# Block-sparse attention with float32 products and gathered key blocks, split units for experts 0 and 1, and seven block products in the first layer of experts 3 to 7

## The chip, the cores and the metric

The kernel runs on one core of a Trainium2 chip. The core has a matrix engine (TensorE, PE in the rows; its weight loads are PEld), a vector engine (DVE), a scalar engine (ACT), a general one (POOL), a synchronization engine (SP) and 16 DMA engines. DMAs are issued from the queues of SP, ACT and POOL. The metric is device time in microseconds, lower is better.

## What is computed

Sparse attention over 4 batches, 8 heads, 768 positions of 64 features, then a layer of 8 experts of which each of the 3072 rows takes its top two:

```python
    mask = np.abs(blk_i - blk_j) <= window          # blocks of 32, window 1
    mask = mask | (blk_i == 0) | (blk_j == 0) | (blk_i == n_blocks - 1) | (blk_j == n_blocks - 1)
    for qb in range(n_blocks):                      # 24 blocks
        for kb in sampled_blocks[qb]:               # 3 each
            mask[qb * block:(qb + 1) * block, kb * block:(kb + 1) * block] = True
    scores = np.where(mask, scores, -1000000000.0)
...
    attn = attn / (np.sum(attn, axis=-1, keepdims=True) + 1e-09)
    return np.matmul(attn, v).astype(np.float32)
...
    noisy_logits = logits + noise_scale * noise
    top2 = np.argpartition(-noisy_logits, 2, axis=1)[:, :2]
...
            h = np.maximum(x[mask] @ w1[e], 0.0)
            out[mask] += top2_w[mask, k, None] * (h @ w2[e])
```

`x` is the attention's output with 512 features a row; `w1[e]` is 512 x 1024, `w2[e]` 1024 x 512. So a query block of the middle sees at most eight key blocks (first, last, three neighbours, three sampled), and the two end blocks of queries see all 24. A wrong choice of expert changes a whole row, so the scores need more than float16's accuracy.

## The kernel before

**Attention** (`Attention`) goes through 192 steps: 4 batches x 8 heads x 6 row tiles of 128. Each step treats all 768 keys; the mask is added by extra rows of the contraction. Values of float32 are split into a float16 high and low half, and products are made of two or three float16 products. A step has these parts: `max_mm` (L227) computes rough scores of 128 rows x 768 keys in two matmuls, and `max_red` (L234, DVE) takes the row maximum; `exp` computes exact scores turned the other way (keys on partitions) in four matmuls (L255, L256) and `exp` of them on ACT (L257) as 32-bit patterns, of which `halve` (L262, DVE) makes two float16 numbers each; `av` multiplies them with the values, 18 matmuls of 64 or 65 columns (L288). After six steps of a head `av_end` copies, normalizes and rounds the result (L300 to L317, ACT, DVE, POOL). Loading and splitting q, k and v (L160 to L198) uses ACT and POOL and DMA transposes on SP's queue.

**Router** (`Router.run`) runs as a list of small steps that are drawn one by one between the attention's; per batch it computes the gates, takes the top two, counts places with matmuls against a triangle of ones, and scatters (row, weight) into a table in DRAM (`slots`, L647).

**Experts** (`Experts`). A unit is a stretch of one expert's rows: first 640 rows of expert 0 out of batches 0 to 2, which can start while batch 3 is still being routed, then 224 rows of expert 0 from batch 3, then 816 rows for each of experts 1 to 7. For a unit, `meta` and `indices` read the table, `gather` fetches rows (POOL), `xpose` turns them with a DMA transpose (SP), `mm1` computes the first layer in 8 groups of 12 products (high-high, high-low, low-high of four input blocks; L816, 408 columns for units of 816), ACT and DVE make the rounded half `hh` and the rest `hl` (L821, L822), `mm2` the second layer, 24 matmuls of 512 columns for each 128 rows (L836), and `finish` scales, adds what the other expert has left there (`gather_prev`, L782) and scatters to `out` (L864, L866). Of the rows beyond the last full 128, `mm2` computes the transpose (L845) and `turn` turns it with float32 transposes (L855). Weights come as 8 pieces of 512 KB per expert (`load_piece`, SP) and are split by ACT and DVE (L729, L730) during the unit before.

Each engine works through its instructions in the order of the program; the order is written out by hand: `steps` and the final loop call the parts one after the other. An instruction waits for semaphores of those whose data it needs, and what stands behind it on its engine waits too. PSUM has 8 banks; a pool's number of buffers says how far its writer may run ahead of its reader.

## Time and profile before

| | |
|---|---|
| time, median of 3 runs | 1052.07 us (1046.19 to 1056.2) |
| span of the profiled execution, first to last instruction | 1028.6 us |
| busy share of the span: PE, DVE, ACT, POOL | 87%, 55%, 37%, 35% |
| granted TensorE clock, mean | 0.971 |
| bytes moved by DMA | 156.40 MB |

Of the profiled execution the span alone is given, no time beside it: the timed runs include what lies around the first and the last instruction, the span does not. An average over the whole span mixes two stages, attention and the experts, so the views by window are of more use. A matmul's busy time includes its way through the array; how fast matmuls follow each other is read from their starts.

### The profile page before, as it was taken

What the parts mean: (1) busy time and instruction counts of PE and PEld (TensorE: products, weight loads), DVE (VectorE), ACT (ScalarE), POOL (GpSimd) and SP (SyncE); (2) the same over time, 40 slices, a digit from 0 to 9 for tenths busy, and PEclk for the clock granted to TensorE, in tenths of its full rate; (3) what the DMA queues carried; (4) which work ended last, traced back from release to release, by engine and by line L of the source; (5) the groups of instructions that cost most, each with busy time, mean ns of one, the idle gap of its engine ahead of it and who ended that gap; (6) DMA issues with size and microseconds to landing.
All of it is one profiled execution on the core that took longest, in us unless ns stands there. A gap on an engine that the chain in (4) does not pass through costs nothing. (4 is left out here: it accounts for less than half of the span.)

```text
span 1028.6 us, 20575 instructions
## 1 busy us (share of the span) xinstructions
PE 891.4 (87%) x8413; PEld 529.1 (51%) x8413; DVE 563.1 (55%) x1039; ACT 377.1 (37%) x754; POOL 355.9 (35%) x399
## 2 busy tenths in 40 slices
PE   3788897779878878997899999989989999899993
PEld 1465565556555545653645455545544544454551
DVE  7699989979988977464123333323323323233320
ACT  2466666556656645432113123122122221221200
POOL 3142322542255253333360251342512513512211
PEclk9899999999999999998999999999999999999997
DMA  8988986899989766736957376295494483653200
GB/s 183 182 171 183 219 196 159 154 164 179 182 178 167 144 133 145 200 85 176 165 130 199 109 174 184 90 196 168 131 184 141 124 214 104 182 144 110 69 34 33
DMA packets 238073, 156.40 MB, mean 152 GB/s; under 512 B 172577, under 2 KB 213793, under 8 KB 237968
## 3 DMA queue, kind: packets, MB, share of 16 engines
q1 hardware_dynamic: 206816, 91.45, 44.1%
q0 software_dynamic: 14256, 39.58, 13.2%
q10 hardware_dynamic: 16896, 23.95, 8.6%
q8 instruction: 68, 1.11, 0.5%
q14 instruction: 37, 0.30, 0.1%
HBM read 79.62 MB, written 26.32 MB: 103 GB/s over the span
## 5 line engine op out<-in xcount | busy, mean ns | idle before, releaser
L257 ACT ACTIVATE p<-pe 128x384 int32<-128x384 f32 x384 | 183.0, 491 | 152.8 <-PE pe L256 125.7
L822 DVE SCALAR_TENSOR_TENSOR hl<-ph,hh 128x408 f16<-128x408 f32 (+2 forms) x136 | 75.6, 560 | 211.2 <-ACT hh L821 177.0
L866 POOL DMA_INDIRECT out_dram<-y,mt x56 | 73.0, 1304 | 323.9 <-DVE y L864 196.4
L234 DVE TENSOR_REDUCE m<-pm 128x1 f32<-128x768 f32 x192 | 181.6, 948 | 1.4 <-PE pm L227 1.4
L821 ACT ACTIVATE hh<-ph 128x408 f16<-128x408 f32 (+2 forms) x136 | 66.2, 492 | 301.9 <-PE ph L816 210.2
L227 PE MATMUL pm<-k,q 88*128 88x384 f16 x384 | 98.5, 340 | 67.8 <-DVE m L234 42.6
L262 DVE TENSOR_SCALAR p<-p 128x1536 f16<-128x1536 uint16 x192 | 124.7, 650 | 45.9 <-ACT p L257 44.0
L288 PEld LDWEIGHTS <-p 128*128 128x128 f16 x3456 | 130.4, 100 | 25.8 <-issue 4.7
L255 PE MATMUL pe<-q,k 128*128 128x384 f16 x384 | 128.7, 335 | 7.7 <-ACT p L257 4.4
L256 PE MATMUL pe<-q,k 128*128 128x384 f16 x384 | 127.9, 333 | 6.7 <-DMA q<-qb 6.7
L288 PE MATMUL po<-vx,p 128*128 128x65 f16 x1152 | 125.3, 197 | 1.8 <-issue 1.4
L288 PE MATMUL po<-vb,p 128*128 128x65 f16 x1152 | 125.8, 196 | 0.9 <-issue 0.9
L288 PE MATMUL po<-vl,p 128*128 128x64 f16 x1152 | 125.5, 195 | 0.0
L836 PEld LDWEIGHTS <-hh 128*128 128x128 f16 x768 | 75.0, 98 | 93.8 <-issue 8.8
L864 DVE SCALAR_TENSOR_TENSOR y<-py,mt,pv 128x512 f32<-128x512 f32 x48 | 36.0, 751 | 153.9 <-PE py L836 145.0
L816 PE MATMUL ph<-xta,w1hb 128*128 128x408 f16 x512 | 110.9, 339 | 9.6 <-DVE hl L822 8.7
L816 PE MATMUL ph<-xtb,w1ha 128*128 128x408 f16 (+1 forms) x448 | 95.3, 334 | 14.2 <-DVE hl L822 12.3
L227 PEld LDWEIGHTS <-q 88*128 88x128 f16 x384 | 37.9, 100 | 122.1 <-issue 96.7
L816 PEld LDWEIGHTS <-w1ha 128*128 128x128 f16 x576 | 57.4, 100 | 52.9 <-issue 18.4
L836 PE MATMUL py<-w2ha,hh 128*128 128x512 f16 x192 | 73.9, 385 | 4.9 <-DVE y L864 3.9
L816 PEld LDWEIGHTS <-w1hb 128*128 128x128 f16 x512 | 50.2, 98 | 49.7 <-issue 12.3
L836 PE MATMUL py<-w2la,hh 128*128 128x512 f16 x192 | 73.8, 384 | 0.3 <-issue 0.3
(172 smaller groups left out, 1404.3 us busy)
## 6 DMA issues: line engine op xcount, KB each, us to landing
wraw<-in_moe_w_dram SPq DMA_DIRECT2D x64, 512.0 KB
q<-q SPq DMA_DIRECT2D x32, 192.0 KB
raw_v<-in_v_dram ACTq DMA_DIRECT2D x16, 384.0 KB
out_dram<-zero ACTq DMA_DIRECT2D x8, 768.0 KB
x_rows<-x SPq DMA_DIRECT2D x16, 384.0 KB
raw_k<-in_k_dram ACTq DMA_DIRECT2D x14, 384.0 KB
raw_q<-in_q_dram ACTq DMA_DIRECT2D x14, 384.0 KB
k<-k SPq DMA_DIRECT2D x17, 192.0 KB
```

The lines of the kernel that those rows point to most:

```text
L227: self.nc.tensor.matmul(pm[:, c, 0:384], r["q3"][0:K, h, t, :], r["k2"][0:K, h, 3 * c:3 * c + 3, :], start=True, stop=True)
L234: self.nc.vector.tensor_reduce(self.st[g]["m", h][:, t:t + 1], pm[:, :, 0:384], axis=AX.XY, op=ALU.max)
L255: nc.tensor.matmul(pe[:, 0:384], r["k1"][:, h, c, :], r["q1"][:, h, t, :], start=True, stop=False)
L256: nc.tensor.matmul(pe[:, 0:384], r["k2"][:, h, c, :], r["q2", h][:, t, :], start=False, stop=True)
L257: nc.scalar.activation(p32[:, t].rearrange("p t c -> p (t c)"), pe[:, 0:384], AF.Exp, scale=0.125)
L262: self.nc.vector.tensor_scalar(p.rearrange("p t c w -> p (t c w)"), p32.bitcast(U16).rearrange("p t c -> p (t c)"), HC, None, op0=ALU.mult)
L288: self.nc.tensor.matmul(o, p[:, t, :, w], v, start=first and i == 0, stop=last and i == 2, skip_group_check=True)
L816: nc.tensor.matmul(ph[:, b, 0:m], w[wt][:, kb, fs], r["xt"][:, kb, a, o:o + m], start=i == 0, stop=i == last)
L821: nc.scalar.activation(hv, ph[:, b, 0:m], AF.Relu)
L822: nc.vector.scalar_tensor_tensor(self.hl[:, f, o:o + m], ph[:, b, 0:m], 0.0, hv, op0=ALU.max, op1=ALU.subtract)
L836: nc.tensor.matmul(py, h[:, f, o], w[x][:, f, :], start=i == 0, stop=i == last)
L866: nc.gpsimd.indirect_dma_start(out=self.out, out_offset=bass.IndirectOffsetOnAxis(ap=r["mt"][0:m, c, 0:1], axis=0), in_=y[0:m], in_offset= ...
```

## The change

**Attention** is written anew. The host lays the inputs out in other orders (queries and keys turned, 32-row blocks together, values with their neighbours side by side); this is outside the time measured. The work is a list of 64 items: per batch 12 of kind "q" (row tile t of 128 queries = 4 blocks, and f, half of the heads) and 4 of kind "g" (the 64 queries of the first and last block against all 768 keys for two head pairs). All matmuls and transposes of attention are float32, with no split.

- `prefetch_k`: POOL copies the three sampled key blocks of each query block behind the keys, 128 x 128 each, from an address held in a register. `prefetch_v`: SP loads the neighbours' values in one DMA and each sampled block in a DMA of 64 KB at a register's address, 11 on average per row tile. A sampled block that is seen already gets weight 0 (`blocks`, `weigh`).
- `scores`: for each of 4 heads and 4 query blocks a matmul of 64 rows, 32 stationary columns and 192 moving ones (three neighbours, three sampled), and 4 matmuls of 64 columns for the end blocks. A head of a pair uses the upper or the lower 64 partitions and a bank of its own.
- `soft`: row maxima (DVE) and `exp` (ACT, 4 of 256). `turn`: PE transposes them, 8 of 128 x 128 in the same banks, copied out by DVE and ACT. `av`: 32 matmuls of 68 columns, each for 32 queries. `norm`: three DVE operations. `high`, `low`: float16 halves on ACT and POOL. `turn_x`: PE instead of DMA transposes the rows for the router, DVE copies them; they go through the one bank `ps_o` that `av` uses.
- The row store, the zero fill of the output and all loads are issued by SP; the zero fill moves from attention to the first unit of the experts.

**Units.** Experts 0 and 1 both have a unit of 640 rows out of the first three batches and one of 224; the short ones come third and fourth. The units of 640 and 224 that come first for their rows (0 and 2) do not read the output back.

**Seven products.** For experts 3 to 7 the first layer's four input blocks and 816 rows are taken as 2 x 2 blocks and multiplied with seven products in place of eight: 28 products of 6 matmuls of 408 columns. DVE and ACT make sums of weights (`weight_sums`), sums and differences of rows (`row_sums`, `row_differences`, `row_high`, `row_low`) during the unit before, and add the products up (`layer1_fast`). PSUM banks: three "pa", two "pc", two "pd", one "pr". The output DMAs of one unit no longer wait for each other.

On PE in the middle of attention, rows of before (`k`, `q` are halves of keys and queries, `p` the exponentials, `vx`, `vl`, `vb` the values' halves):

```order
L227 LDWEIGHTS q_2318
L227 MATMUL pm<-k_100,q_2318 128x384
L255 LDWEIGHTS k_1827
L255 MATMUL pe<-q_1980,k_1827 128x384
L256 LDWEIGHTS k_102
L256 MATMUL pe<-q_2317,k_102 128x384
L288 LDWEIGHTS p_2466
L288 MATMUL po<-vx_104,p_2466 128x65
L288 LDWEIGHTS p_2466
L288 MATMUL po<-vl_110,p_2466 128x64
L288 LDWEIGHTS p_2466
L288 MATMUL po<-vb_107,p_2466 128x65
```

and of the change, one q item (`kk` keys, `q` queries, `va` and `vb` values, `ptr` turned exponentials; `x16` counts equal neighbours):

```order
L298 MATMUL ps<-r_ident,p 128x128 x8
L225 MATMUL ps<-kk_106,q 32x192 x16
L225 MATMUL ps<-kk_106,q 128x64 x4
L320 MATMUL po<-va_99,ptr 32x68 x4
L320 MATMUL po<-vb_102,ptr 32x68 x4
L320 MATMUL po<-va_99,ptr 32x68 x4
L320 MATMUL po<-vb_102,ptr 32x68 x4
```

The two rough matmuls and the four exact ones of a row tile are gone; 16 narrow ones and 8 transposes stand in their place for four heads, and the 18 value matmuls of a tile become 32 with 32 rows of output each.

On DVE in the middle of attention, before (`m` maxima, `p` exponentials, `rc` and `xr` normalization):

```order
L305 RECIPROCAL rc<-rc 128x6
L308 TENSOR_TENSOR xr<-xo,rc 128x384
L262 TENSOR_SCALAR p_4207<-p_4177 128x1536
L234 TENSOR_REDUCE m<-pm 128x1
L262 TENSOR_SCALAR p_4241<-p_4210 128x1536
L234 TENSOR_REDUCE m<-pm 128x1
L262 TENSOR_SCALAR p_4278<-p_4248 128x1536
```

and in the change, about two items (`ps` scores or their transposes, `po` the bank of the outputs, `r_xT` the turned rows):

```order
L302 COPY ptr<-ps 128x512
L391 COPY r_xT<-po 128x1024
L271 TENSOR_REDUCE m<-ps 128x2 x2
L327 TENSOR_SCALAR rc<-po 128x4
L328 RECIPROCAL rc<-rc 128x4
L330 TENSOR_TENSOR xr<-po,rc 128x256
L302 COPY ptr<-ps 128x512
L271 TENSOR_REDUCE m<-ps 128x2 x2
L307 MEMSET ptr 32x4x32
```

A row tile and head had one maximum over 768 and one scaling over 1536 halves; an item of four heads has one copy of 512, two maxima over 512 and three operations of normalization, every second one a copy of 1024 too.

On DVE in the first layer of an expert, before (`hl` low halves, `w2la` weights' low halves, `gi` indices, `y` output rows):

```order
L822 SCALAR_TENSOR_TENSOR hl<-ph,hh 128x408 x4
L730 SCALAR_TENSOR_TENSOR w2la<-wraw,w2ha 128x1024
L752 TENSOR_SCALAR gi<-mt 128x6
L752 TENSOR_SCALAR gi<-mt 48x1
L822 SCALAR_TENSOR_TENSOR hl<-ph,hh 128x408 x12
L864 SCALAR_TENSOR_TENSOR y<-py,mt,pv 128x512
```

and in the change, first layer of a unit with seven products (`pa`, `pc`, `pd` banks, `ta`, `tc` partial sums, `xf` row sums, `w_...` weights):

```order
L980 TENSOR_TENSOR tc<-pa,tc 128x408
L963 SCALAR_TENSOR_TENSOR hl<-tc,hh 128x816
L980 TENSOR_TENSOR tc<-pd,tc 128x408
L963 SCALAR_TENSOR_TENSOR hl<-pa,hh 128x408
L980 TENSOR_TENSOR ta<-pc,ta 128x408
L963 SCALAR_TENSOR_TENSOR hl<-tc,hh 128x816
L963 SCALAR_TENSOR_TENSOR hl<-ta,hh 128x408
L825 SCALAR_TENSOR_TENSOR w_11313<-wraw,w_11313 128x1024
L836 TENSOR_TENSOR xf<-xta 128x816
```

Sixteen low halves with little between them become additions, low halves, weight halves and row sums in one sequence.

The diff, cut to the parts above:

```diff
-        pm = self.ps_m.tile([P, 2, 512], F32, name="pm")
-        for c in range(2):
-            self.nc.tensor.matmul(pm[:, c, 0:384], r["q3"][0:K, h, t, :], r["k2"][0:K, h, 3 * c:3 * c + 3, :],
-                                  start=True, stop=True)
...
-        nc.tensor.matmul(pe[:, 0:384], r["k1"][:, h, c, :], r["q1"][:, h, t, :], start=True, stop=False)
-        nc.tensor.matmul(pe[:, 0:384], r["k2"][:, h, c, :], r["q2", h][:, t, :], start=False, stop=True)
-        nc.scalar.activation(p32[:, t].rearrange("p t c -> p (t c)"), pe[:, 0:384], AF.Exp, scale=0.125)
...
-        for t in range(self.T):
-            first, last = c == 0 and t == 0, c == self.T - 1 and t == self.T - 1
-            for i, (o, w, v) in enumerate(((po[:, t, :], 1, vh[:, h, c, :]), (po[:, t, 0:D], 1, vl[:, h, c, :]),
-                                           (po[:, t, :], 0, vb[:, h, c, :]))):
-                self.nc.tensor.matmul(o, p[:, t, :, w], v, start=first and i == 0, stop=last and i == 2,
-                                      skip_group_check=True)
...
+    def prefetch_k(self, b, t):
+        nc, kk = self.nc, self.kk[b % 2]
+        js = self.real(t)
+        v = self.numbers(self.ri, t, mybir.EngineType.Pool, self.NB - 1)
+        flat = kk.rearrange("p n c -> p (n c)")
+        for j in js:
+            for n in range(3):
+                nc.gpsimd.tensor_copy(kk[:, self.row(t, j) + n], flat[:, bass.ds(v[j, n] * P, P)])
...
+        part = lambda x: x.rearrange("p (j c) -> p j c", j=J)[:, js[0]:js[-1] + 1]
+        nc.sync.dma_start(va[0:96, js[0]:js[-1] + 1, 0:HD], part(self.vw[b, t]))
+        v = self.numbers(self.mi, t, mybir.EngineType.SP, self.NB)
+        vv = self.vx[b].rearrange("(n p) c -> n p c", p=32)
+        for j in js:
+            for n, d in enumerate((va[96:128, j], vb[0:32, j], vb[32:64, j])):
+                nc.sync.dma_start(d[:, 0:HD], vv[bass.ds(v[j, n], 1)].rearrange("o p c -> (o p) c"))
...
+    def scores(self, it):
...
+        q = self.st["q", b, t]
+        self.st[it, "s"] = [self.bank() for _ in range(2)]
+        s = [x.rearrange("p (e c) -> p e c", e=2) for x in self.st[it, "s"]]
+        for e in range(2):
+            p = 2 * f + e
+            for j in range(self.NJ):
+                blk = min(max(t * self.NJ + j - 1, 0), NB - 3)
+                for par in range(2):
+                    w = kk[head(par), blk:blk + 3, p]
+                    step = (self.row(t, self.slot(t, j)) - blk) * P
+                    w = bass.AP(tensor=w.tensor, offset=w.offset, ap=[list(w.ap[0]), [step, 2]] + [list(a) for a in w.ap[1:]])
+                    mm(s[par][32 * j:32 * j + 32, e, 0:192], q[head(par), p, 32 * j:32 * j + 32], w)
+        for e in range(2):
+            p = 2 * f + e
+            for par in range(2):
+                mm(s[par][:, e, 192:256], q[head(par), p, :], kk[head(par), 0:NB:NB - 1, p])
+    def soft(self, it):
...
+        m = self.sm.tile([P, 2, 2], F32, name="m")
+        p = self.st[it, "p"] = self.pp.tile([P, 4, 256], F32, name="p")
+        for par in range(2):
+            nc.vector.tensor_reduce(m[:, par], s[par].rearrange("p (e c) -> p e c", e=2), axis=AX.X, op=ALU.max, negate=True)
+        for par in range(2):
+            for e in range(2):
+                nc.scalar.activation(p[:, 2 * e + par], s[par][:, 256 * e:256 * e + 256], AF.Exp, bias=m[:, par, e:e + 1])
+    def av(self, it):
...
+        va, vb = self.st["v", b, t]
+        o = self.st[it, "o"] = self.psum()[:, 0:4 * W].rearrange("p (h w) -> p h w", w=W)
+        for h in range(4):
+            for x, v in ((0, va), (1, vb)):
+                for j in range(self.NJ):
+                    nc.tensor.matmul(o[32 * j:32 * j + 32, h], d[:, h % 2, h // 2, x, 32 * j:32 * j + 32],
+                                     self.values(v[:, self.slot(t, j)], 4 * f + h), start=h == 0 and x == 0,
+                                     stop=h == 3 and x == 1, skip_group_check=True)
+    def norm(self, o, n):
+        nc, D = self.nc, self.D
+        rc = self.sm.tile([P, n], F32, name="rc")
+        nc.vector.tensor_scalar(rc, o[:, :, D], 1e-9 / XS, None, op0=ALU.add)
+        nc.vector.reciprocal(rc, rc)
+        x = self.xp.tile([P, n, D], F32, name="xr", bufs=3)
+        nc.vector.tensor_tensor(x, o[:, :, 0:D], rc[:, :, None].to_broadcast([P, n, D]), op=ALU.mult)
+        return x
...
+    def turn_x(self, xT, b, t):
+        nc = self.nc
+        x = self.x_tile(b, t).rearrange("p k a c -> p (k a) c")
+        o = self.psum().bitcast(F16).rearrange("p (c k) -> p c k", c=2 * self.NP)
+        for c in range(2 * self.NP):
+            nc.tensor.transpose(o[:, c], x[:, c], self.ident16)
+        nc.vector.tensor_copy(xT[:, t].rearrange("p k a c -> p (k a) c"), o)
...
-        self.units = [(0, 0, CA), (E, 0, CB)] + [(e, e, C) for e in range(1, E)]
+        self.units = [(0, 0, CA), (1, 1, CA), (E + 1, 1, CB), (E, 0, CB)] + [(e, e, C) for e in range(NH, E)]
+PRODUCTS = [(int(a), int(b)) for a, b in ("01 11 02 06 12 21 07 16 05 17 04 15 03 14 22 27 26 31 13 24 36 25 37 35 "
+                                           "32 34 23 33").split()]
+HOOKS = (3, 6, 10, 13, 17, 20, 23, 27)
...
+    def weight_sums(self, e, i):
...
+        a = self.st["wraw", e, i].rearrange("p (s c) -> p s c", s=4)
+        c = self.st["ws", e, i] = self.sp.tile([P, 4, 2 * P], F32, name="ws")
+        tt = lambda x, y, z, op: nc.vector.tensor_tensor(x, y, z, op=op)
+        tt(c[:, 0], a[:, 3], a[:, 2], ALU.add)
+        tt(c[:, 1], c[:, 0], a[:, 0], ALU.subtract)
+        tt(c[:, 2], a[:, 0], a[:, 3], ALU.subtract)
+        tt(c[:, 3], a[:, 1], c[:, 1], ALU.subtract)
...
+    def layer1_fast(self, u, hook):
...
+        t = lambda i: (lambda s, a: tb[:, s, a, i])
+        terms = {1: (0, x(0, 0)), 2: (1, x(1, 0)), 3: (6, x(1, 1)), 4: (2, t(2)), 5: (3, t(0)), 6: (4, t(3)), 7: (5, t(1))}
...
+        for n, (g, p) in enumerate(PRODUCTS):
+            w = self.w1b[self.units[u][1], g]
+            slot, mv = terms[p]
+            if p in tail:
+                banks[g, p] = self.bank(tail[p])
+            o = banks[g, owner[p]][:, 0:M]
+            i = 0
+            for s in range(2):
+                for wt, a in ((0, 0), (0, 1), (1, 0)):
+                    nc.tensor.matmul(o, w[:, wt, slot, s * P:s * P + P], mv(s, a), start=i == 0 and p in tail,
+                                     stop=i == 5, skip_group_check=True)
+                    i += 1
...
+            if p == 1:
+                once[g] = self.tp.tile([P, M], F32, name="ta")
+                keep(once[g], ba)
+            if p in (6, 7):
+                if g not in both:
+                    both[g] = self.tp.tile([P, 2, M], F32, name="tc")
+                keep(both[g][:, p - 6], bd if p == 7 else ba)
+            if p == 2:
+                tt(once[g], bc[:, 0:M], once[g])
+                self.high(g, 0, M, once[g])
+                later.append((g, 0, M, once[g]))
+            seen = set(PRODUCTS[:n + 1])
+            if p == 4:
+                tt(both[g][:, 0], bd[:, 0:M], both[g][:, 0])
+            if p in (5, 7) and {(g, 5), (g, 7)} <= seen:
+                tt(both[g][:, 1], ba[:, 0:M], both[g][:, 1])
+            if p in (4, 5, 7) and {(g, 4), (g, 5), (g, 7)} <= seen:
+                v = both[g].rearrange("p k c -> p (k c)")
+                self.high(4 + g, 0, C, v)
+                later.append((4 + g, 0, C, v))
+            if p == 3:
+                self.high(g, M, M, ba[:, 0:M])
+                later.append((g, M, M, ba[:, 0:M]))
...
+        for p in r.setdefault("done", []):
+            self.tc.declare_no_dep(d.ins, p.ins, reason="a unit has every row once")
```

## Rows read from the trace of the kernel before

**Rows 1.** The page: span.
```profile
span 1028.6 us, 20575 instructions
```
**Rows 2.** Windows by stage: start:end, us, busy and (count) per engine, clock, DMA, GB/s.
```profile
60.00:400.00 340.00, 280.23 (x4169) 194.51 (x4168) 309.26 (x607) 206.99 (x466) 132.40 (x166) 0.98 0.85 169
452.00:487.50 35.50, 29.72 (x124) 12.47 (x122) 14.91 (x21) 9.43 (x11) 17.96 (x27) 0.90 0.59 137
585.20:1012.00 426.80, 410.63 (x2623) 215.88 (x2620) 136.83 (x199) 91.50 (x143) 136.81 (x120) 0.98 0.52 138
1012.00:1028.60 16.60, 0.00 (x0) 0.00 (x0) 0.64 (x1) 0.00 (x0) 0.98 (x1) 0.65 0.05 19
```
**Rows 3.** Tiles po and ph: duration ns min/median/max, first and last start (us).
```profile
L288 PE MATMUL po<-vx,p x1152: 190/194/262, 33.6 to 419.5; 128*128 128x65 f16 x192
...
L816 PE MATMUL ph<-xtb,w1ha x448: 256/336/548, 488.0 to 909.8; 128*128 128x408 f16 x128, 128*128 128x224 f16 x22
...
L816 PE MATMUL ph<-xta,w1ha x128: 296/299/474, 419.6 to 452.0; 128*128 128x320 f16 x128
```
**Rows 4.** The page, costliest groups: count, busy us, mean ns, idle before.
```profile
L234 DVE TENSOR_REDUCE m<-pm 128x1 f32<-128x768 f32 x192 | 181.6, 948 | 1.4 <-PE pm L227 1.4
...
L262 DVE TENSOR_SCALAR p<-p 128x1536 f16<-128x1536 uint16 x192 | 124.7, 650 | 45.9 <-ACT p L257 44.0
```
**Rows 5.** Groups by form, DVE.
```profile
L822 DVE SCALAR_TENSOR_TENSOR hl<-ph,hh 128x408 f16<-128x408 f32 x112 | 64.8, 582 | 188.1 <-ACT hh L821 160.8 <-issue 27.3
L864 DVE SCALAR_TENSOR_TENSOR y<-py,mt,pv 128x512 f32<-128x512 f32 x48 | 36.0, 751 | 153.9 <-PE py L836 145.0 <-remote 8.4 <-DVE w2lb L730 0.5
...
L730 DVE SCALAR_TENSOR_TENSOR w2la<-wraw,w2ha 128x1024 f16<-128x1024 f32 x16 | 19.6, 1223 | 1.9 <-ACT w2ha L729 1.5 <-issue 0.4
...
L308 DVE TENSOR_TENSOR xr<-xo,rc 128x384 f32<-128x384 f32 x32 | 17.8, 558 | 2.8
...
L303 DVE TENSOR_SCALAR rc<-xo 128x6 f32<-128x6 f32 x32 | 5.2, 161 | 1.3 <-ACT xo L300 1.3
...
L521 DVE COPY r_lc<-pe 128x192 f32<-128x192 f32 x3 | 1.0, 346 | 0.0
```
**Rows 6.** Timelines of PE: start, us (of merged neighbours), shapes, count; three stretches.
```profile
99.66 0.19 PE L288 MATMUL po<-vx,p 128*128 128x65 f16 x1
99.69 0.19 PE L288 MATMUL po<-vl,p 128*128 128x64 f16 x1
...
513.70 0.60 PE L855 MATMUL pr<-r_ident,yt 128*96 128x128 f32 x4
514.14 0.64 PE L816 MATMUL ph<-xta,w1hb 128*128 128x408 f16 x2
...
586.16 0.85 PE L816 MATMUL ph<-xtb,w1ha 128*128 128x408 f16 x4
...
587.20 0.85 PE L816 MATMUL ph<-xtb,w1ha 128*128 128x408 f16 x4
```
**Rows 7.** Groups by form, ACT.
```profile
L257 ACT ACTIVATE p<-pe 128x384 int32<-128x384 f32 x384 | 183.0, 491 | 152.8 <-PE pe L256 125.7 <-PE pm L227 7.5 <-remote 7.0
...
L821 ACT ACTIVATE hh<-ph 128x224 f16<-128x224 f32 x8 | 2.7, 356 | 16.9 <-PE ph L816 12.3 <-remote 4.6
```
**Rows 8.** Groups by form, POOL.
```profile
L647 POOL DMA_INDIRECT slots<-r_pay,r_sl x48 | 51.5, 1072 | 39.4 <-DVE r_ot L639 30.2 <-issue 7.7 <-DVE r_pay L636 1.2
...
L194 POOL TENSOR_TENSOR ka<-raw_k,ka 128x384 f16<-128x384 f32 x28 | 27.0, 963 | 37.0 <-ACT ka L192 33.0 <-DMA q<-qb 2.7 <-issue 1.2
...
masks.py:197 POOL MEMSET r_ident<- 128x128 f32 x1 | 0.2, 199 | 0.0
```
**Rows 9.** Timeline of SP's queue: start, us that issuing took; two stretches.
```profile
1.23 0.42 SPq L330 DMA_DIRECT2D raw_k<-in_k_dram  x1
...
315.57 1.14 SPq L498 DMA_DIRECT2D x_rows<-x  x1
```
**Rows 10.** The page, DMA queues: packets, MB, share of 16 engines.
```profile
q0 software_dynamic: 14256, 39.58, 13.2%
```

## What the change should do

> **What bounds the kernel now.** I read the stage windows first, then each engine's groups. The last value matmul (L288) starts at 419.5 us and the first expert matmul (L816) at 419.6 [rows 3], so the span of 1028.6 us [rows 1] is 419.5 us of attention, 592.5 us of experts (to 1012.0) and a tail of 16.6 in which PE does nothing [rows 2]. The reader is to see in the window 60:400 which engine is full: DVE is busy 309.3 of 340 us (91%), PE 280.2 (82%), ACT 207.0 (61%). Two DVE groups make nearly all of it: the row maximum L234 (948 ns) and the scaling L262 (650 ns), both 192 times [rows 4], together 306.8 us. Attention is bound by DVE, with PE close behind. In the experts the order is reversed: in 585.2:1012 PE is busy 410.6 of 426.8 us, DVE 136.8 [rows 2]. There PE is the bound, and only fewer columns or fewer stalls shorten it. The timed median, 1052.07 us, lies 23.4 above the profiled span; I add that to every sum.
>
> **Attention, DVE.** The change removes L234 and L262 altogether, and most of the scores: 192 row tiles of 768 keys become 48 items ("q": 128 queries, 4 heads, 256 keys) and 16 items for the queries of the two end blocks ("g"). Prices: a DVE read of PSUM costs 346 ns for 192 elements (L521) and 948 for 768 [rows 4, 5], hence 145 ns + 1.045 ns per element: 680 ns for 512, 546 for 384, 1215 for 1024; the product L308 (558 ns for 384) gives about 425 for 256 [rows 5]. Per q item: one copy of 512 (0.68), two maxima over 512 (1.36), the normalization (two small operations of 0.16 to 0.18 and the 0.43), half of a 1024 copy (0.61): 3.42 us. A third of a g item (two maxima of 384, one small operation, one copy: 1.93) is 0.64. The router, whose work is not changed, has some 50 small DVE operations a batch at 0.16 to 0.2 us, like L303 [rows 5]: 9 us, for three of four batches within attention 27 / 48 = 0.57. Small copies and memsets: 0.25. Sum 4.9 us an item, 48 x 4.9 = 235 us, in place of 306.8 for two groups alone.
>
> **Attention, PE.** Everything is now float32, and no row shows a float32 product; the nearest are the four float32 transposes L855, which take 513.70 to 514.14, 109 ns each for 128 columns, 0.85 ns a column. A float16 column costs 0.42 (six matmuls of 408 in 1.035 us, 172.5 ns each), and a matmul of 65 columns still follows the last after 31 ns [rows 6]. Per item there are 16 score matmuls of 192 columns, 4 of 64, 32 value matmuls of 68, a third of 4 x 384 and 5.3 x 68 for the end blocks: 6380 columns, besides 10.7 transposes (1.16 us) and 4 float16 ones (0.22). One after the other at 0.85 ns that is 6.8 us an item. But a score matmul uses 64 rows and 32 columns of the array, and its neighbours use the others and other PSUM banks or partitions; a value matmul uses 32 columns. If they run side by side (8, 2, 4, 2 and 2 at a time) 1493 columns are left, 2.65 us. The matmuls of before use 128 rows (L227: 88) and all 128 columns (the 128*128 of [rows 6]), so the trace decides nothing. I take the middle of the two ends, 4.7 us: just under DVE.
>
> By the Trainium skill ("TensorEngine Tiling (Array Packing)", Key Properties) tiles of the array load weights and multiply independently and in parallel; no run here shows that yet. By it PE would take 2.65 us and DVE alone would bound; without it, PE bounds at 6.8 (the second rival below).
>
> **Attention, the feeders.** ACT: 384 elements take 491 ns, 224 take 356 [rows 7], so 383 for 256: four exponentials, one copy of 512, one rounding, and shares of the end blocks' work come to 3.5 us, hidden under DVE. POOL copies 264 key blocks of 128 x 128 at a register's address (5.5 an item). The nearest rows are a memset of that size (199 ns) and a two-input operation on 384 elements (963) [rows 8]; I take 0.45 with its register work, nearer the memset: 2.5 us, and 2.5 more for scaling, low halves, weights and the slot DMAs (1.07 us each): 5.0, level with DVE. SP issues about 7.4 DMAs an item, 11 per 128 queries at register addresses. An issue took 0.42 us at the start and 1.14 in full attention [rows 9]; at 0.6 that is 4.4 us. The moved bytes are 6.3 MB of keys, 6.3 of queries, 17.3 of neighbour values, 17.3 of sampled ones, 6.3 stored and about 3 others, 56 MB; queue q0 moved 39.58 MB in 13.2% of 1028.6 us [rows 10], 291 GB/s, so 56 MB want 192 us: hidden if attention takes 260.
>
> **Attention, sum.** DVE was busy 91% when it was the bound; 235 / 0.91 = 258. Before it, 12 us until the keys (1.6 MB, 6 us) and block numbers are there and three items are in flight; before, the first value matmul starts at 33.6 us [rows 3]. After it 8 us for the last item, whose turned rows now go through PE ahead of the first expert matmul: a chain of some eight short operations with their waits. 278 us, against 419.5.
>
> **Experts.** A unit of 816 rows took 71.1 us in the mean of seven (514.1 to 1012.0 [rows 2, 6]). Seven products of half size in place of eight: 168 first-layer matmuls of 408 columns instead of 192, 24 x 0.1725 = 4.1 us less for each of five units [rows 6]. The price is on DVE. Per such unit: 12 additions of 408 (0.58 like L822), the low halves (4 x (0.58 + 1.0 + 0.58)), weight sums (16 of 256, 0.42) and the longer weight splits (0.95 + 1.22 x 2 for each quarter), row sums, differences and low halves (about 12), seven L864 of 0.75 [rows 5]: 54 us in 67, where before it is busy 32%. In the first layer alone 26 us of DVE stand against 29 of PE. The banks (three "pa", two "pc", two "pd") let PE run about four products ahead, so I leave the remaining stalls as large as before, 4 us a unit. The unit of 640 rows takes 68.4 us before (419.6 to 488.0 [rows 3]) for 51.9 of PE work: 26.0 and 25.9. I take 60 for the first (the eight fills of the output, 6.3 MB, move here from attention), 54 for the second, whose rows and weights come under the first, 21 for each short one (18 of work; 26 before, when it waited for the last batch's table). Sum: 60 + 54 + 42 + 71 + 5 x 67 = 562 us, against 592.5. The waits between a unit's output DMAs are declared away; the tail hardly sees it, since the last DMA waits for the last y.
>
> Total: 278 + 562 + 16.6 = 857 us of span, 880 with the 23.4.
>
> **Rivals.**
> *Products in four passes, one at a time (slower).* The kernel before gets its accuracy from float16 halves, three products for one (L816). If the array does the same inside a float32 product with all four, a column costs 4 x 0.42 = 1.69 ns; without overlap an item takes 12.2 us of PE, attention 48 x 12.2 + 20 = 606, the whole 1208 us. It decides from 9.0 us an item (attention 450 us), 1.2 ns a column in series. For it: no row shows overlap. Against it: transposes show half that price. The Trainium skill ("FP8 and Floating Point Precision", TensorE Precision Notes) does state four passes for true float32, with nothing on tiles.
> *PE bounds, still faster.* At 0.85 ns in series 6.8 us an item: 326 + 20 + 562 + 17 + 23 = 948. Four passes side by side, 3.9 us, would be hidden; at half clock 7.8 us: 996. For the half clock: before, PE at 82% was granted 0.98, but 0.90 in 452:487.5 where it stood still [rows 2], and it will stand still in each item.
> *The feeders bound.* POOL copies at 963 ns (5.3 + 2.5 = 7.8 us an item) or SP issues at 1.14 (8.4): 374 to 403 + 20, 996 to 1025 us; at 0.6 a copy, 920.
> *Seven products gain nothing.* DVE at 26 of 29 us holds the banks back and the 4.1 us are lost: 900 us, inside the range.
>
> **Numbers.** 58% for DVE-bound attention near 880 (own range 830 to 930); 20% for PE as a bound that stays under 1040; 10% for the feeders; 12% for the serial four passes. The floor is DVE without loss (235 + 20) and the experts at their PE work (521): 816. So 825 to 1000 leaves out the slow rival, the worst of the feeders and a little below. This kernel can tell about 1% from no change: faster by more 0.85, within 0.03, slower 0.12.
>
> **What would show it.** Right: attention ends near 280 us with DVE above 85% there; value matmuls of one item starting a few tens of ns apart; five units near 67 us with first layers near 31. Wrong: PE above 95% and DVE under 60% in attention (either PE rival, told apart by the start-to-start time of the score matmuls and the granted clock); PE's score matmuls waiting for POOL's key copies or value matmuls for SP's DMAs; first layers of 35 us or more with PE waiting for DVE additions.

## The result, and the profile after

The changed kernel took 921.59 us in the median (919.55 to 921.78), the kernel before 1051.28 beside it; the ratio is 0.8806, 95% interval 0.8745 to 0.8866. In a second comparison on the chip it took 909.72 beside 1032.86, ratio 0.8817 (0.8773 to 0.8860). The forecast was 880, range 825 to 1000. Executions of one kernel lie up to 3% apart here (the kernel before: 1026 to 1056), so stages are compared inside profiles, and times only with runs taken beside them.

The profiled execution took 921.78 us, its span is 919.8. The page's first lines, and its line on the queue that brings instructions (packets, MB, share of 16 engines):

```profile
span 919.8 us, 25194 instructions
PE 823.3 (90%) x10119; PEld 520.1 (57%) x10119; DVE 538.3 (59%) x1151; ACT 357.6 (39%) x666; POOL 380.5 (41%) x662
...
q8 instruction: 81, 1.33, 0.7%
```

Windows by stage (columns as in [rows 2]): attention in full flow, its last stretch, all of the experts, the five units with seven products:

```profile
60.00:330.00 270.00, 225.51 (x5201) 172.00 (x5189) 165.59 (x480) 135.92 (x301) 140.61 (x375) 0.94 0.69 165
330.00:351.90 21.90, 14.30 (x281) 12.36 (x282) 8.62 (x26) 3.23 (x8) 6.43 (x9) 0.58 0.90 173
351.90:903.70 551.80, 536.95 (x3616) 301.56 (x3615) 327.33 (x547) 184.66 (x289) 203.95 (x176) 0.98 0.60 160
588.30:903.70 315.40, 315.19 (x2062) 167.00 (x2060) 224.91 (x335) 125.17 (x185) 118.75 (x92) 1.00 0.52 143
```

Attention ends at 351.9 us (419.6 before, [rows 3]); the forecast was 278. The experts take 551.8 (592.5 before; forecast 562), the tail 16.1 (16.6). So the experts came out a little better than forecast and attention ended 74 us later. And DVE, which was to be full, is busy 165.6 of 270 us (61%; 91% before, [rows 2]), PE 225.5 (84%). No engine is full. The last window shows the opposite picture: PE 315.19 of 315.40 us, at full clock.

The values' and the turned scores' groups (duration min/median/max, first and last start):

```profile
L320 PE MATMUL po<-va,ptr x1536: 219/223/323, 26.5 to 343.6; 128*32 128x68 f32 x192
...
L391 DVE COPY r_xT<-po x24: 673/692/692, 56.9 to 351.1; 128x1024 f16<-128x1024 f16 x24
...
L271 DVE TENSOR_REDUCE m<-ps x96: 672/681/692, 18.6 to 328.5; 128x2 f32<-128x512 f32 x96
L302 DVE COPY ptr<-ps x48: 675/682/693, 22.2 to 336.4; 128x512 f32<-128x512 f32 x48
```

`va` has 768 matmuls in the program and 1536 records here: a float32 product appears as two. PE's timeline in the middle of attention (start, us, shapes, count, idle time before and its releaser):

```profile
149.71 0.96 PE L225 MATMUL ps<-kk,q 64*32 64x192 f32 x16
150.60 0.33 PE L320 MATMUL po<-va,ptr 128*32 128x68 f32 x8
150.74 0.30 PE L320 MATMUL po<-vb,ptr 128*32 128x68 f32 x8
150.86 0.30 PE L320 MATMUL po<-va,ptr 128*32 128x68 f32 x8
...
152.11 0.27 PE L346 MATMUL pog<-va,pgt 96*64 96x68 f32 x1
152.66 0.30 PE L346 MATMUL pog<-va,pgt 96*64 96x68 f32 x2 [0.28 <-issue]
153.43 0.28 PE L346 MATMUL pog<-va,pgt 96*64 96x68 f32 x2 [0.46 <-issue]
154.17 1.05 PE L346 MATMUL pog<-va,pgt 96*64 96x68 f32 x27 [0.46 <-issue]
155.15 1.09 PE L298 MATMUL ps<-r_ident,p 128*128 128x128 f32 x8
```

Two things are to be seen. Eight value records take 0.12 us: four start 7 ns apart (one for each 32 columns of the array), the next four 59 ns after the first. That is 0.87 ns a column for each record, four records at a time. By the Trainium skill ("TensorEngine Tiling (Array Packing)", Key Properties) tiles load and multiply in parallel; the trace agrees, and the second experiment shows it by undoing it. Then, at 152 us, matmuls that need nothing new come two at a time with 0.45 us of nothing between. The profile puts that idle time down to "issue": it sees no semaphore that PE waits for. POOL's timeline has this beside it:

```profile
151.35 0.99 POOL L716 DMA_INDIRECT slots<-r_pay,r_sl  x1 [0.16 <-issue]
152.34 0.09 POOL L715 MEMSET r_spacer<- 1x1 f32 x1
152.65 0.98 POOL L716 DMA_INDIRECT slots<-r_pay,r_sl  x1 [0.22 <-issue]
153.66 0.64 POOL L166 TENSOR_SCALAR q<-q 128x512 f32<-128x512 f32 x1
```

PE's waits in attention, from 60 to 330 us (total us, times, longest):

```profile
PE po L320 <- issue: 25.2, 39, 3.2
PE pog L346 <- issue: 6.8, 18, 0.5
PE po L662 <- DVE xr L330: 4.0, 3, 1.9
```

No such idle time has a place in the prediction. Summed over the records from 30 us to attention's end, PE has 38.3 us of idle time before matmuls that wait for no semaphore, in 68 pieces: 55 pieces under 0.6 us (20.1 us), 50 of them within half a microsecond of an indirect DMA of POOL, and 13 longer ones (18.2 us, the longest 3.2). The kernel before has 2.3 us of it. The experiments start there.

### The profile page after: what moved, and what is told of

Its sections match the earlier page's. It is cut to its first block, busy times and chain, and to the rows that moved or that the text cites. A ratio compares the mean times of both kernels' runs of the same rounds, so it can differ in the third digit from the quotient of the medians.

```text
span 919.8 us, 25194 instructions
## 1 busy us (share of the span) xinstructions
PE 823.3 (90%) x10119; PEld 520.1 (57%) x10119; DVE 538.3 (59%) x1151; ACT 357.6 (39%) x666; POOL 380.5 (41%) x662
## 3 DMA queue, kind: packets, MB, share of 16 engines
q8 instruction: 81, 1.33, 0.7%
## 4 chain that ended last, share of the span: by engine, by line
PE 76%; DVE 7%; issue 6%; DMA 3%; another core or an unknown queue 3%; ACT 2%; SPq 1%; POOL 1%; POOLq 0%; DVEq 0%
PE pc L1038 24%; PE pa L991 9%; PE ps L225 9%; PE po L320 7%; PE pd L991 5%; PE ps L298 4%; PE pa L952 4%; PE pc L1047 3%; PE pog L346 3%; PE pc L991 2%; PE pd L952 2%; DVE m L271 2%; PE ps L286 2%; PE po L390 2%
## 5 line engine op out<-in xcount | busy, mean ns | idle before, releaser
L1038 PE MATMUL pc<-w,hh 128*128 128x512 f16 x768 | 230.1, 381 | 0.0
L1038 PE MATMUL pc<-w,hl 128*128 128x512 f16 x384 | 146.3, 381 | 0.0
L991 PEld LDWEIGHTS <-w 128*128 128x128 f16 x840 | 82.2, 98 | 63.1
L274 ACT ACTIVATE p<-ps,m 128x256 f32<-128x256 f32 x192 | 75.4, 475 | 70.0 <-DVE m L271 59.0
L271 DVE TENSOR_REDUCE m<-ps 128x2 f32<-128x512 f32 x96 | 61.8, 684 | 44.5 <-PE ps L225 37.7
L225 PE MATMUL ps<-kk,q 64*32 64x192 f32 (+1 forms) x1920 | 75.3, 329 | 4.7 <-issue 4.0
L894 POOL DMA_INDIRECT xg<-x_rows,gi x56 | 68.7, 1227 | 23.2 <-issue 15.3
L320 PE MATMUL po<-vb,ptr 128*32 128x68 f32 x1536 | 63.9, 233 | 13.9 <-issue 13.5
L825 DVE SCALAR_TENSOR_TENSOR w<-wraw,w 128x1024 f16<-128x1024 f32 (+1 forms) x58 | 65.1, 1126 | 18.9 <-ACT w L821 16.2
L186 POOL COPY kk<-kk 128x128 f32 x264 | 64.7, 298 | 25.5 <-PE ps L225 18.7
L821 ACT ACTIVATE w<-wraw 128x1024 f16<-128x1024 f32 (+1 forms) x58 | 56.4, 975 | 5.1 <-DMA wraw<-in_moe_w_dram 4.8
```

What stands on the lines that cost most here:

```text
L186: nc.gpsimd.tensor_copy(kk[:, self.row(t, j) + n], flat[:, bass.ds(v[j, n] * P, P)])
L225: mm = lambda o, l, r: nc.tensor.matmul(o, l, r, start=True, stop=True, skip_group_check=True)
L271: nc.vector.tensor_reduce(m[:, par], s[par].rearrange("p (e c) -> p e c", e=2), axis=AX.X, op=ALU.max, negate=True)
L274: nc.scalar.activation(p[:, 2 * e + par], s[par][:, 256 * e:256 * e + 256], AF.Exp, bias=m[:, par, e:e + 1])
L320: nc.tensor.matmul(o[32 * j:32 * j + 32, h], d[:, h % 2, h // 2, x, 32 * j:32 * j + 32], self.values(v[:, self.slot(t, j)], 4 * f + h), st ...
L821: self.nc.scalar.activation(hi, t, AF.Copy, scale=WS)
```

## The experiments

"Attention's end" is the first matmul of an expert in the profile; "short" and "long" is PE's idle time without a wait (before matmuls that wait for no semaphore) from 30 us to that end, in pieces under and over 0.6 us, summed over the records.

| kernel | attention's end | short, us (pieces) | long, us (pieces) |
|---|---|---|---|
| changed kernel, first and second profile | 351.9, 355.0 | 20.1 (55), 20.3 (56) | 18.2 (13), 16.5 (10) |
| maxima twice | 388.1 | 12.4 (35) | 11.2 (6) |
| value matmuls tile by tile | 399.6 | 5.6 (21) | 2.7 (3) |
| wide value matmuls | 329.7 | 5.8 (18) | 4.4 (4) |
| few values loaded | 334.5 | 12.5 (32) | 11.4 (10) |
| no scatter | 317.2 | 0.1 (1) | 14.0 (8) |
| no scatter, few values | 298.1 | 1.2 (4) | 5.4 (3) |
| plain DMAs of POOL | 341.7 | 2.7 (9) | 33.4 (18) |
| plain DMAs of SP | 342.9 | 2.4 (8) | 20.8 (11) |

### Is DVE the bound? Each maximum twice

```diff
         for par in range(2):
-            nc.vector.tensor_reduce(m[:, par], ...)
+            for i in range(2):
+                nc.vector.tensor_reduce(m[:, par], ...)
```

> Every row maximum of a q item is taken twice (96 more reductions of 0.68 us on DVE, 65 us in all); the output is unchanged. If DVE bounds attention, as the prediction had it, the first expert matmul moves from 351.9 us to 405 to 417. If PE and its stalls set the pace and DVE's 54% is cover, it moves by less than 15 us.

Single run, 953.92 us. Attention's end moved to 388.1, by 36 us, between the two expectations. DVE (third pair) is busy 71% of the time, and the clock fell to 0.86 (0.94 in the changed kernel's window):

```profile
60.00:360.00 300.00, 237.20 (x5154) 179.46 (x5151) 212.59 (x550) 136.84 (x297) 137.84 (x371) 0.86 0.62 139
```

PE's longest waits for DVE in this window:

```profile
PE po L663 <- DVE xr L331: 9.1, 3, 4.0
PE po L391 <- DVE xr L331: 7.6, 7, 1.4
PE po L321 <- DVE r_ef L638: 7.4, 2, 3.7
```

DVE is neither the bound nor cover: of 65 us added, 36 show. From 30 us to attention's end PE's waits for DVE grew from 14 to 46 us. Nearly all are for normalization (`xr`, `xe`) and for router operations (`r_ef`, `r_lc`), which stand behind the maxima in DVE's order; only 1.3 us are for a maximum itself.

### Do narrow matmuls overlap only in the right order?

```diff
-        for h in range(4):
-            for x, v in ((0, va), (1, vb)):
-                for j in range(self.NJ):
+        for j in range(self.NJ):
+            for h in range(4):
+                for x, v in ((0, va), (1, vb)):
                     nc.tensor.matmul(o[32 * j:32 * j + 32, h], ...)
```

> The same 32 value matmuls of an item in another order: all eight of one stretch of 32 output rows, then the next stretch, so that neighbours in the order use the same 32 columns of the array. If matmuls side by side overlap only with their neighbours in the order, an item's 64 records follow each other at 59 ns in place of four every 59 ns: 3.8 us in place of 0.95, 48 x 2.8 = 136 us more, attention's end near 485 and the whole near 1055. If each part of the array has a queue deep enough, or if the overlap in the records is not real, nothing changes (within 5 us).

The same matmuls, in an order in which neighbours need the same columns of the array, now follow each other one by one:

```profile
149.68 0.28 PE L320 MATMUL po<-vb,ptr 128*32 128x68 f32 x2
149.80 0.28 PE L320 MATMUL po<-va,ptr 128*32 128x68 f32 x2
149.91 0.28 PE L320 MATMUL po<-vb,ptr 128*32 128x68 f32 x2
150.03 0.31 PE L320 MATMUL po<-va,ptr 128*32 128x68 f32 x4
150.15 0.31 PE L320 MATMUL po<-vb,ptr 128*32 128x68 f32 x4
```

Two records in 0.12 us where there were eight; only where one stretch ends and the next begins do two run side by side (the lines with x4). An item's value matmuls take 3.1 us in place of 0.95 where nothing stops them (3.8 expected). In this single run of 963.73 us attention's end moved by 47.7 us and not by 136: PE's own pace (from start to start, without the gaps) grew by 79 us, from 267.1 to 346.5 after 30 us, and 30 us of the idle time without a wait went away, now that PE asks for instructions more slowly. PE became the bound: 302.67 of 320 us busy in the window 60:380. So the overlap is real, the order in the program decides it here, and the idle time shrinks when PE goes more slowly.

### Too many short instructions? Value matmuls of twice the width

```diff
-        for h in range(4):
+        for h in (0, 2):
...
-                    nc.tensor.matmul(o[32 * j:32 * j + 32, h], d[...], self.values(v[...], 4 * f + h), ...)
+                    w = v[:, self.slot(t, j)].rearrange(...)[:, 4 * f + h:4 * f + h + 2]
+                    nc.tensor.matmul(o[32 * j:32 * j + 32, h:h + 2], d[...], w, ...)
```

> Two heads' values in one matmul of 136 columns, with the weights of the first of the two: the second head's weights are left out, so its rows of the output are others. The columns are as many as before, the instructions of the value matmuls half as many. If the PE stalls without a wait (38 us between 30 and 352) come from too many short instructions, they fall by a quarter to a half and attention ends at 333 to 343 us, the whole at 903 to 913. If only columns count, the end stays within 3 us of 351.9.

893.23 us, ratio 0.8599 (0.8561 to 0.8638) against 0.8806 and 0.8817 of the changed kernel; attention's end 329.7. The columns are the same, and 28 of 38 us of idle time without a wait are gone, more than the quarter to half expected; 9 us came back as waits for the values' DMAs (60 to 310 us):

```profile
PE po L321 <- issue: 7.1, 12, 1.6
PE po L321 <- DMA va<-in_vx_dram: 5.5, 4, 2.0
PE pog L347 <- issue: 4.9, 9, 1.1
PE po L321 <- DMA vb<-in_vx_dram: 3.4, 3, 1.5
```

### Is the DMA traffic hidden? Values loaded for batch 0 alone

```diff
+        if b * self.T + t >= 6:
+            return
         js = self.real(t)
         part = lambda x: ...
         nc.sync.dma_start(va[0:96, ...], part(self.vw[b, t]))
```

> Values of neighbours and sampled blocks are loaded for batch 0 alone; later batches multiply with the old ones (their outputs are others). About 26 MB of DMA and 200 issues on SP less after 90 us. If the long single stalls of PE (0.5 to 3.2 us, some 11 us after 90 us) wait for instructions behind a busy DMA, they go, the short ones of 0.2 to 0.5 us beside POOL's indirect DMAs stay, and attention ends at 335 to 343 us. If the transfers are hidden and the stalls have another cause, it stays within 3 us of 351.9.

892.49 us, ratio 0.8601 (0.8569 to 0.8633); attention's end 334.5. The traffic between 60 and 315 us is down to 77 GB/s from 165, and PE hardly waited for these transfers before: in its waits they do not appear. Attention is 17 us shorter without them all the same. The long idle pieces went from 18.2 to 11.4 us; the short ones fell too (20.1 to 12.5), which was not expected.

### POOL's indirect DMAs

```diff
         for t in range(T):
             for k in range(2):
-                nc.gpsimd.memset(self.spacer, 0.0)
-                s = nc.gpsimd.indirect_dma_start(out=self.table, ...)
+                if last:
+                    nc.gpsimd.memset(self.spacer, 0.0)
+                    s = nc.gpsimd.indirect_dma_start(out=self.table, ...)
...
```

> The 36 indirect DMAs with which POOL writes the tables of batches 0 to 2 during attention are left out (the experts then gather blank rows for them and their output is others; only attention is compared). If PE's short stalls without a wait (some 25 us, each within half a microsecond of such a DMA) are caused by them, they go, the granted clock stays above 0.95 between 290 and 330 us, and attention ends at 318 to 328 us. If the coincidence is one of place only, it ends within 5 us of 351.9.

The short pieces vanished (0.1 us left, of 20.1), the long ones stayed (14.0), and attention ended at 317.2, just under the 318 to 328 expected. The clock did not do as expected: from 290 us to the end it is 0.83, not above 0.95, with PE busy 15.8 of 27.2 us there. The waits from 60 to 300 us and the window in full flow:

```profile
PE po L320 <- issue: 6.6, 6, 2.1
PE po L320 <- DMA va<-in_vx_dram: 4.3, 2, 3.1
```

```profile
60.00:300.00 240.00, 210.72 (x5354) 163.86 (x5353) 167.43 (x488) 137.19 (x305) 103.51 (x305) 0.96 0.71 189
```

36 DMAs of 1 KB, on an engine that PE never waits for, cost attention 35 us, about a microsecond each. From 30 us on, 24 us of gaps are gone (38.3 to 14.1), and PE's own pace is 19.5 us faster (267.1 to 247.6). Most of that is gap too: a gap is counted from the modelled end of the matmul before it, and from start to start the short pieces make 34 us, not 20; besides, the mean clock from 30 us on is 0.95 in place of 0.92. 9 us came back as waits for other engines and DMAs (15.8 to 24.8). Without the traffic and without these DMAs together:

> Both left out: the 36 indirect DMAs of batches 0 to 2 and the loads of values after batch 0 (the output is another). If the two are separate causes of PE's stalls without a wait, under 5 us of these are left and attention ends at 298 to 306 us (317.2 without the DMAs alone, 334.5 without the loads alone). If one cause stands behind both, the gains do not add and it ends at 311 to 318. If the prediction's bound by DVE were what remains, it would come to 280 with DVE above 85%.

Attention ended at 298.1 us, so the gains add (35 + 17 would give 300). 6.6 us of idle time without a wait remain (under 5 expected), and now one engine is nearly full, and it is PE, with 93% (DVE 76%):

```profile
60.00:280.00 220.00, 205.59 (x5353) 161.45 (x5352) 167.66 (x483) 136.56 (x306) 102.99 (x305) 0.97 0.29 88
```

The profile is that of a run of 863.2 us, where the four took 845 to 866, so 298.1 is if anything late. The records give PE's own pace here, starts to starts without gaps: 243.2 us for the 47 items after 30 us, 5.2 us an item, of which about: scores 1.4, values 1.2, transposes 1.0, end blocks 1.1, turned rows and router 0.4.

### What of the DMA disturbs PE?

```diff
-                s = nc.gpsimd.indirect_dma_start(out=self.table, out_offset=..., in_=pi[:, t, k, :], in_offset=None)
+                if last:
+                    s = nc.gpsimd.indirect_dma_start(out=self.table, out_offset=..., in_=pi[:, t, k, :], in_offset=None)
+                else:
+                    n = 2 * (b * T + t) + k
+                    s = nc.gpsimd.dma_start(self.table[OVBASE + n * P:OVBASE + n * P + P], pi[:, t, k, :])
```

> In place of the 36 indirect DMAs POOL issues plain DMAs of the same 128 pieces of 8 bytes to fixed places at the end of the table (the output is another; only attention is compared). If it is POOL's making of descriptors that slows PE, the stalls of 0.2 to 0.5 us stay (15 to 25 us in all) and attention ends at 340 to 353. If it takes the indirect form, they go and it ends at 315 to 322 as without the DMAs.

The second kernel has `nc.sync` in place of `nc.gpsimd` in the last line, and its plain DMAs are not entered in the list of scatters.

> The same 36 plain DMAs of 128 pieces of 8 bytes, issued from SP's queue (the output is another; only attention is compared). If the many small writes themselves slow PE, whoever issues them, the short stalls stay (15 to 25 us) and attention ends at 340 to 353. If it is POOL's part in them, the short stalls are under 3 us and it ends at 315 to 330, the upper end if SP's loads get late behind their waits.

Single runs, 912.28 and 903.26 us. The short pieces are gone in both (2.7 and 2.4 us), so the trains of 0.45 us gaps belong to the indirect form on POOL, not to small writes and not to POOL's issuing as such. But neither ended where this should have brought it (315 to 322, and 315 to 330). With plain DMAs of POOL the long pieces grew to 33.4 us, and with SP's the value loads got late:

```profile
PE po L320 <- issue: 19.5, 15, 4.1
PE ps L225 <- issue: 8.4, 4, 3.8
```

```profile
PE po L320 <- DMA va<-in_vx_dram: 11.7, 9, 5.0
PE po L320 <- issue: 8.3, 8, 2.1
```

(the first two lines from the kernel with POOL's plain DMAs, the others with SP's; both 60 to 320 us).

What the long pieces are can be read from the packets of the instruction queue, q8, in the same traces. A packet has 16 KiB (1.33 MB in 81). There is one for every 252 of PE's 20412 records (matmuls, weight loads, its sequencer's), and 69 for the 17341 with wide matmuls. In the changed kernel's first profile 11 of the 13 long pieces (16.1 of 18.2 us) end at records that lie whole multiples of 256 apart, to within one, and each ends 1.3 to 1.7 us after such a packet has landed; the other two lie beside indirect DMAs of POOL. So most of the long idle time is PE out of instructions until the next block is there. Counted in this way late blocks make 12.1 us in the second profile, 5.0 with few values, 1.3 with wide matmuls, none tile by tile, 14.0 without the scatter, 5.4 without scatter and values, and 31.4 and 20.8 with the plain DMAs of POOL and SP. A packet starts, in the median, 1.8 us after PE has entered the block before it, 0.8 with few values and 2.2 with POOL's plain DMAs; but 0.8 also in the kernel before, whose DMA queues move 169 GB/s, so it is not the bytes alone. What delays the packets stays open.

### Eight products in experts 3 to 7

```diff
     def fast(self, u):
-        return u >= FAST
+        return False
     def weight_sums(self, e, i):
-        if e < FAST - 2 or i >= 4:
-            return
+        return
```

and likewise no row sums, no additional weights.

> Experts 3 to 7 take the plain first layer of eight products (192 matmuls of 408 columns), with no sums of weights or rows; the rest, the banks and the order of loads stays. If the seven products are worth their columns alone, each first layer goes from 29.0 to 33.1 us: 5 x 4.1 = 20.5 us, the whole near 942. If the stalls of the kernel before (first layers of 33 to 42 us) come back with the plain form, units take 71 to 74 us in place of 63: 962 to 977. If DVE's additions cost something now hidden in the second layer, less than 20 us are lost.

932.09 us, ratio 0.9015 (0.8969 to 0.9061); the changed kernel's is 0.8817 in the later comparison. The difference of 0.0198 of 1033 us is 20.5 us, with the two intervals 14 to 27. PE's windows of a first layer (the instructions of L991 in the changed kernel, of L955 with eight products; busy and count of PE and of its weight loads):

```profile
588.30:617.30 29.00, 29.00 (x168) 16.32 (x167) 1.00 0.55 156
```

```profile
643.80:677.00 33.20, 33.16 (x192) 18.69 (x191) 1.00 0.46 136
```

4.1 us per layer, five times, agrees with the difference. And the plain layer takes 33.1 us here without a stall, where the kernel before needed 33 to 41 (37.1 in the mean of its seven). So of the 8 us that a unit of 816 rows won (71.1 to 63.1), the seven products give 4.1, and the other 4 come from what else changed there (loads, banks, splits), which no run takes apart. Not all is gain: expert 2, whose unit prepares the first sums, has a first layer of 40.0 us, and 35.8 when there are no sums; its unit takes 73.9 us (71 to 75 in the other runs with sums) and 69.8. In the two profiles the five layers' 20.7 us are therefore some 16 net.

### What lies around the span

The kernel before, unchanged.

> The kernel before, unchanged, to see what lies between a run's time and its span. If 23 us lie around the span, as the prediction added, the run takes about 1052 us with a span near 1029. If the profiled execution was only a faster one than those timed, time and span differ by about 2 us, as 921.78 and 919.8 of the changed kernel do, and the spread sits in the span: 1030 to 1056.

It took 1035.82 us with this span:

```profile
core 0: 1034.0 us, clock 0.969
```

In this execution 1.8 us lie around the span, not 23.4. The second run of the changed kernel:

> The changed kernel, unchanged, as the measure for the others, since the kernel before took 1035.8 us beside them and 1051.3 beside the first. If executions differ by as much here, 905 to 922 us; attention's end within 3 us of 351.9. The eight products' 932.1 us would then be 10 to 27 us more; 20.5 if nothing but the columns of five first layers is paid.

909.72 us (907.96 to 921.1). Its profile is that of the run of 921.1 us (span 919.1, attention's end 355.0, 3.1 us later than in the first): it repeats the first profile's stages, not its median.

## Why the prediction was right or wrong

**The total** fell into the range, and in part by luck: it was to be DVE-bound near 880, and DVE was not the bound. Against the span of 857 the profile has 919.8: attention +74, experts -10, tail 0. Of the 63 us, 21.6 were covered by an error of the other sign:

**The 23.4 us around the span** do not exist. The step set the span of one execution against the median of others and took the difference for a constant. The two are 1.8 to 2.0 us apart in each execution; the profiled one was shorter than those timed.

**"DVE was busy 91% when it was the bound; 235 / 0.91 = 258"** is the step that failed. The prices were good: 0.68 us forecast for the copy and the maxima, 682 and 681 ns measured; 425 ns for the product, 425 measured. Only the copy of 1024 (L391) was sized from float32 rows, 1.215 us for 0.69, which lowers DVE's sum from 235 to 223; measured are 210 in all. The conclusion failed: DVE is 61% busy, and doubling its maxima showed 36 of 65 us. What set the pace in its place is PE's own work and PE's idle time without a wait, below.

**PE at 4.7 us an item**, the middle of two ends, was mis-sized: 5.2 at its own pace (no scatter, few values). Both ends of it were wrong. Matmuls do run side by side, but a float32 product has two records of 0.87 ns a column, 1.7 ns in all; the transposes, from which 0.85 was taken, have one. So "four passes side by side", 3.9 us in the rivals, covers the columns and transposes, and the rest are 0.1 to 0.25 us at each change of shape, some six an item. The Trainium skill ("FP8 and Floating Point Precision", TensorE Precision Notes) states the four passes, and the trace agrees: 1.7 ns are four times 0.42. "TensorEngine Tiling (Array Packing)", Key Properties, also states that a change of tiling mode drains the engine; the trace has such a gap of 0.2 us between the scores and the values (7 to 59 ns within the values). That sentence stood in the page from which the other rule was taken, and it was left out of the sum.

**The serial rival** (1208 us) did not come: its condition of 9.0 us an item needed matmuls one at a time, and the tile-by-tile order, which makes the value matmuls so, still ends at 399.6. **The feeders** did not bound as told: POOL's key copies take 298 ns (0.45 forecast), and PE waits for one of POOL's results for 0.8 us. ("At 0.6 a copy, 920" is a slip: 48 x 5.8 + 20, with the experts, the tail and the 23.4, gives 900.) ACT's exponentials of 256 took 475 ns, 383 forecast, and stayed hidden. **PE as the bound, still faster** is the rival that came nearest, by its time (948, 996 at half clock) and by its engine, but not as written, since PE is full only when the idle time is taken away.

**What no step contained** is idle time of PE without a wait. The chain of the sum from 12 to 278 measured: first value matmul at 26.5 us (12 forecast), 317.3 from there to the last (258), 8.1 to the first expert matmul (8). So 14.5 of the 74 us lie in the start, where PE's first scores run at 8.3 us; no run takes it apart. The 59 us between 317.3 and 258 stand against 38 of gaps without a wait and 24 by which PE's own pace is slower beside them (267.1 against 243.2); without their causes the same stretch takes 260.8 us. That this is near the 258 forecast is chance: PE is 93% busy there and DVE 76%. "Hidden if attention takes 260", said of the 56 MB, was wrong in the same way: PE hardly waited for the transfers, and without most of the values attention is 17 us shorter.

**The clock** was named in a rival only ("it will stand still in each item"; in the window that it cites for this, PE was in fact busy 29.7 of 35.5 us): 0.94 in 60:330 and 0.58 from 330 to the end, after the stalls, where PE waits for the last items' chains.

**Experts:** 562 forecast, 551.8 measured. The long units took 56.4 and 56.3 (60 and 54), the short ones 23.9 and 26.1 (21 each), expert 2 73.9 (71), the five others 63.1 (67). The wrong term is "the remaining stalls as large as before, 4 us a unit": there are none in these five units (315.19 of 315.40 us busy). The whole 4.1 us of the seven products came through in each, with DVE busy 71% of the time beside it, and some 4 us went again in expert 2, where the first sums are made. The rival that they gain nothing fell.

**The signs** that were to tell the cases apart did half their work: value matmuls tens of ns apart and fast units near 67 came (59 ns and 63 us), but neither "DVE above 85%" nor "PE above 95%" did. A case in which no engine is full had no sign of its own.

## What to carry to other kernels

When a bound engine is relieved, the next time is not set by the fullest engine alone: put the engines' order into the sum, and ask of every engine how many instructions a microsecond it must be fed; here blocks of 256 instructions came late where PE ran through short matmuls. Many short matmuls side by side pay off if neighbours in the order use different tiles of one shape; group them by shape, and prefer wide ones where columns allow, since 28 us of idle time went here with half the value matmuls. Before adding a constant from a time and a span, check that both are of the same execution.

## What the hardware showed

- POOL's indirect DMAs disturb PE: during most of them (about 1 us each) PE, when it runs short float32 matmuls, starts a few and then has 0.4 to 0.5 us of nothing. 36 of them cost 35 us. In the experts, where matmuls of 408 columns follow each other at 172 ns, POOL issues 105 of them from 560 to 905 us and PE has 0.2 us of such gaps.
- Long gaps without a wait, 0.8 to 4 us, are for the most part late blocks of instructions: 16.1 us in the changed kernel, 5.0 without most of the value loads, 1.3 with half the value matmuls. The Trainium skill ("Runtime: NRT & Kernel Launch", Instruction fetch mechanics) has PE's instructions fetched by DMA in blocks of 16 KiB (256 instructions) and calls the cost mostly hidden. The trace agrees on the blocks: 1.33 MB in 81 packets on the instruction queue, and gaps at multiples of 256 records. On the cost the measurement decides: from 30 us to attention's end PE enters 49 blocks, and 11 of them made it wait 0.8 us or more, 16.1 us in all. No run moved the fetches alone; that they cause these gaps rests on where and when the gaps end.
- A float32 copy of 512 elements from PSUM takes 682 ns on DVE, a float16 one of 1024 elements, also from PSUM, 692.
